# A Mamba-2 scan feeding a hard-swish MLP: the last chunk's mixing in halves, a sum of weights moved, a state sum left out

## The chip, the cores and the metric

The kernel runs on one core of a Trainium2 chip. The metric is the device time of one execution in microseconds (us). A core has five engines with a queue of instructions each: PE (TensorE, matrix products), DVE (VectorE), ACT (ScalarE), POOL (GpSimd) and SP (SyncE, which issues most DMA transfers here). Each runs its own queue in order and waits on semaphores for the others. PE's results go to PSUM, which has eight banks; everything else is in SBUF.

## The reference

A chunked state-space scan over 4 batches x 8 heads x 768 tokens (head size 32, state size 16), whose result is turned to 3072 tokens x 256 and put through an MLP with a hard-swish between its products. The inputs x, a, B and C are float32, the two weights float64.

```python
for c in range(nc):
    cum = np.cumsum(la, axis=-1)
    L = np.exp(cum[:, :, :, None] - cum[:, :, None, :]) * causal
    CB = np.einsum('bhin,bhjn->bhij', Cc, Bc)
    y_intra = np.einsum('bhij,bhjd->bhid', CB * L, xc)
    y_inter = np.einsum('bhin,bhnd->bhid', Cc, state) * np.exp(cum)[..., None]
    y[:, :, sl] = y_intra + y_inter
    state = decay_full * state + np.sum(Bx, axis=2)
...
h = x @ w_in
g = h * np.clip(h + 3.0, 0.0, 6.0) / 6.0
return g @ w_out
```

The state after the last chunk is used by nothing.

## The kernel before

The 768 tokens are taken in NC = 6 chunks of 128, all batches at once, so that a chunk has 512 columns. The main loop at the end of the kernel has a block k for each chunk: it multiplies chunk k through the MLP, and between those products it places the scan of chunk c = k + 1 and the preparation of chunk ahead = k + 2. The order of the instructions on each engine is the order of the calls in the code; it is written out by hand.

**The scan of a chunk.** A chunk is cut in two halves a of 64 tokens, and an inner step runs from half 0 to half 1. `scores(c)` makes C times B for both (tile cb), and then calls `into_state`, which multiplies x by B with its decays (tile bs), one sum for each half, into the banks of y (line L555). `multiply(c)` first has ACT copy the second half's sum to the tile adds (`take`, L571), then DVE multiplies cb into the decays L (L584), and between them `new_state` makes the state between the halves (mid). `renew(c)` makes the state that the next chunk starts from, out of mid and adds; it isn't called for the last chunk. `mix(c, parts)` multiplies L by x for four heads at each part u (L610), and at the end adds what the state between the halves gives (`from_state`, L516). On PE a mixing is 128 small matmuls of L610 and 32 of L516, each with its weight load, since a float32 product is made of two. Then `split_y(c)` cuts the result y into the parts high (ACT, L671), low (DVE, L674) and gap (DVE, L677), from which the first product of the MLP is made.

**A block of the MLP, k of 1 to 5.** For each of 16 slices f of the hidden width, `lead` multiplies the gaps (L683) and then scales its bank: for an even f on ACT (L699), for an odd one on DVE (L696). `follow` adds the products of high and low (L683 too), and ACT and DVE make the hard-swish gT of it (L706, L707). A lead stands two slices ahead of its follow. The first two leads of the next block are put at the end of the block before: in block 0 ahead of its last two out-products, in blocks 1 to 4 at unit 12.

The second product, g @ w_out, has a form with seven products in place of eight, which needs sums of quarters of g (made by POOL, L779) and four sums of quarters of w_out. `weight_sums` makes the latter on DVE, one at each `next(sums)` (L761, 128 x 1024 each), in the order t3, t2, t4 and t1 in place; each but the first uses an earlier one. Block 0 makes its second product the plain way (`first_out`, L734) while the weights still come in. In blocks 1 to 4 `wide_units` makes it in units with a yield between them; after a unit, by its number i, the loop puts in the steps of the scan. Its tiles are wa, wb and wc (L860), a unit has 8 or 16 matmuls. Block 5 uses `out_units` (oa and ob, L793).

**What stands where before.** In block 0: after the out-products (i, b) = (2, 3) come scores, multiply and renew of chunk 1, decays of chunk 2, and two sums of w_out; after (3, 1) come mix and split_y of chunk 1 (`results`), then the third sum, and decays. The fourth sum is made in block 1. In blocks 1 to 4: scores and multiply after unit 2; after unit 6 mix and split_y together, apart from chunk TURN = 3 (block 2), where the first part of mix is put after unit 6 and the second, with split_y, after unit 7. Unit 7 is the second part of a product into wb; its code also has DVE turn back a quarter of the result (L874). For block 4 c = 5 and ahead = 6, so that nothing is loaded or prepared there.

The nested conditions of the loop after unit 6, with the names as above:

```python
                if i == 6 and c == TURN:
                    mix(c, (0,))
                if i == (7 if c == TURN else 6):
                    results(c, (1,) if c == TURN else range(2))
```

Of the kernel before, what the change touches and what calls it, by code (L numbers as in the profile page):

```python
# [21 lines left out]
def kernel(  # L22
# [29 lines left out]
    NC = S // P  # L52
# [34 lines left out]
    TURN = 3  # L87
# [290 lines left out]
    def diff_exp(c, b):  # L378
        if c not in Ls:
            new_decays(c)  # L380
        nc.scalar.activation(Ls[c][:, b], ds.pop((c, b)), AF.Exp)
# [139 lines left out]
    def own_banks(c):  # L521

        both = [ps_y.tile([P, 2, NB, HT], FP32, name=f"y{u}", tag=f"y{u}") for u in range(2)]
        ys[c] = {(0, u): both[u][:, 0] for u in range(2)}
        sps[c] = [both[a if c else 1 - a][:, 1] for a in range(2)]
        if c:
            from_state(c, 0)

    def scores(c):

        bT, cT, _ = bTs[c]
        cbs[c] = [ps.tile([P, NB, 2, HT], FP32, name="cb", tag=f"f{q}") for q in range(NQ)]
        if c not in ys:
            own_banks(c)
        for b in range(NB):
            for a, rows in enumerate(HALF):  # L540
                for q in range(NQ):
                    pair = slice(32 * q, 32 * q + 32)
                    nc.tensor.matmul(  # L543
                        out=cbs[c][q][rows, b], lhsT=bT[pair, b, rows],
                        rhs=cT[pair, b, :, rows], start=(b == 0), stop=True,
                        tile_position=(32 * q, a * HT), skip_group_check=True)
        into_state(c, 0, 1)

    def into_state(c, *halves):
        xt, bs = xts[c], bss[c]  # L550
        for b in range(NB):
            for q in range(NQ):
                hs = slice(b * NH + 2 * q, b * NH + 2 * q + 2)
                for a in halves:
                    nc.tensor.matmul(  # L555
                        out=sps[c][a][32 * q:32 * q + 32, b],
                        lhsT=bs[HALF[a], hs].rearrange("s h n -> s (h n)"),
                        rhs=xt[HALF[a], hs].rearrange("s h d -> s (h d)"),
                        start=(c == 0 and b == 0), stop=True, tile_position=(a * HT, 32 * q),
                        skip_group_check=True)  # L560

    def new_state(t, sp, old):
        for u in range(2):
            ds_ = slice(u * D, (u + 1) * D)
            nc.vector.scalar_tensor_tensor(
                out=t[:, :, ds_], in0=sp[:, :, ds_], scalar=parity[:, u:u + 1],
                in1=old[:, :, ds_], op0=ALU.mult, op1=ALU.add)

    def take(c):
        adds[c] = att.tile([P, NB, 2 * D], FP32, name="adds", bufs=1)  # L570
        nc.scalar.copy(out=adds[c], in_=sps[c][1])  # L571

    def multiply(c):

        take(c)
        mids[c] = mid = att.tile([P, NB, 2 * D], FP32, name="mid", bufs=1)
        if c == 0:
            for t in range(2):
                nc.scalar.activation(
                    mid[:, :, t * D:(t + 1) * D], sps[c][0][:, :, t * D:(t + 1) * D], AF.Copy,  # L580
                    scale=parity[:, t:t + 1])
        for q in range(NQ):
            hs = slice(2 * q, 2 * q + 2)
            nc.vector.tensor_tensor(  # L584
                out=Ls[c][:, :, hs], in0=Ls[c][:, :, hs], in1=cbs[c][q], op=ALU.mult)
            if c and q == 1:
                new_state(mid, sps[c][0], tmps[c])
# [349 lines left out]
    def results(c, parts=range(2)):  # L937
        mix(c, parts)
        split_y(c)
# [18 lines left out]
    def weights(i, n):  # L958
        for _ in range(n):
            next(parts[i], None)  # L960
# [63 lines left out]
    for k in range(NC):  # L1024
        gTs[k] = ffn.tile([P, NF, TB], FP32, name="gT")
        c, ahead = k + 1, k + 2
        if k == 0:
            for f in range(NF):
                mlp_in(k, f)
                for i in weave.get(f, []):  # L1030
                    weights(i, 1)
                if f in (6, 8):
                    diff_exp(c, f // 2 - 3)
            load_bc(ahead)
            weights(NP + 1, 1)
            weights(NP + 3, 1)
            weights(NP + 2, 3)
            sums = weight_sums()
            for i in range(NP):
                for b in range(NB):  # L1040
                    first_out(b, i, c)
                    if (i, b) == (0, 0):
                        weights(NP + 3, 1)
                        weights(NP + 2, 1)
                        weights(NP + 3, 3)
                        rows(ahead)
                    elif (i, b) == (1, 0):
                        for j in range(NP - 1):
                            high_w(j)
                        for j in range(2):  # L1050
                            low_w(j)
                            gap_w(j)
                    elif (i, b) == (2, 0):
                        turn(c, 1)
                        wake(c)
                        turn(c, 0)
                        low_w(2)
                        gap_w(2)
                        high_w(NP - 1)
                        for p in range(2):  # L1060
                            conceal(ahead, p)
                    elif (i, b) == (2, 3):
                        scores(c)
                        multiply(c)
                        renew(c)
                        decay_ends(ahead, 0)
                        decay_ends(ahead, 1)
                        next(sums)
                        next(sums)
                    elif (i, b) == (3, 1):  # L1070
                        results(c)
                        next(sums)
                        decay_ends(ahead, 2)
                        load_x(ahead)
            rows(ahead + 1)
            continue
        for f in range(NF):
            if f == 0:
                if ahead < NC:
                    load_bc(ahead)  # L1080
                if 1 < k and c < NC:
                    carry(c)
                turns = turn_parts(c) if c < TURN else iter(())
            if f + 2 < NF:
                lead(k, f + 2)
            follow(k, f)
            if k == 1:
                if f in (0, 2):
                    low_w(NP - 1, f // 2)
                if f in (4, 6):  # L1090
                    gap_w(NP - 1, f // 2 - 2)
                if f in (1, 3):
                    decay(c, NB - 1, range(f // 2 * HU, (f // 2 + 1) * HU))
                if f == 3:
                    ends(c, NB - 1)
                    from_start(c)
                    carry(c)
            if f in (4, 8) and ahead < NC:
                conceal(ahead, f // 4 - 1)
            if f in (5, 7, 8):  # L1100
                next(turns, None)
            if f == 9 and c < TURN:
                turn(c, 1)
            if f in (4, 8, 12):
                g_sums(k, f // 2 - 2)
        for i, _ in enumerate((wide_units if c < NC else out_units)(k)):
            if i == 0:
                g_sums(k, NJ - 2)
                if k == 1:
                    next(sums)  # L1110
            if c < NC:
                if i == 1 and c == NC - 1:
                    own_banks(c)
                if i == 2:
                    scores(c)
                    multiply(c)
                    if c < NC - 1:
                        renew(c)
                if ahead < NC and 2 <= i < 6:
                    decay_ends(ahead, i - 2)  # L1120
                if i == 6 and c == TURN:
                    mix(c, (0,))
                if i == (7 if c == TURN else 6):
                    results(c, (1,) if c == TURN else range(2))
                    if ahead < NC:
                        load_x(ahead)
                        from_start(ahead)
                    if ahead + 1 < NC:
                        rows(ahead + 1)
                if i == 9 and TURN <= ahead < NC:  # L1130
                    turn_all(ahead)
                if i == 12:
                    lead(c, 0)
                    lead(c, 1)
# [30 lines left out]
```

## Time and profile before

| what | value |
|---|---|
| median of 3 runs | 347.82 us (347.5 to 348.46) |
| the profiled execution: time / its span | 349.42 us / 347.7 us |
| mean granted PE clock | 0.995 |
| PE busy (matmuls) | 335.3 us, 96% of the span |
| DVE / ACT / POOL busy | 220.1 / 173.5 / 141.5 us |
| chain that ended last, shares | PE 89%, DVE 5%, DMA 3%, the rest 3% |
| DMA | 24.89 MB, mean 72 GB/s |

The span runs from the first to the last instruction, the execution's time takes in what lies around it. "Busy" is the time in which an engine had an instruction of its own at work. The chain is followed back from the last instruction, at each step to what released it. "issue" stands for time in which an engine waited for nothing that the profile shows. The page's row of the granted clock, one digit for each of 40 slices of 8.7 us, beside the shares of PE:

```
PE   6799999998999999999999999999999979999996
PEclk9999999999999999999999999999999989999999
```

A digit is a tenth; 9 is 90% or more. By the cut at each block's first wide product, blocks 1, 2 and 3 take 51.55, 51.93 and 51.57 us.

### The profile page before, as it was taken

The numbers are of one execution on the slowest core, as the hardware profiler recorded it, in microseconds if no ns is written. First come the engines' busy times: TensorE is split into PE (matmuls) and PEld (weight loads), VectorE is DVE, ScalarE is ACT, GpSimd is POOL, SyncE is SP. The second block draws the span as 40 slices with busy tenths as digits, with TensorE's granted clock in tenths as the row PEclk, the third lists the DMA queues.
The fourth block names the chain that finished last, engine by engine and source line by source line (L and its number), as shares of the span: only waits on it lengthen the run. The fifth ranks groups of instructions, "written<-read, shape, count | busy, mean of one in ns | idle before, by whom it ended". The sixth has DMA issues, their size and how long they took to land.

```text
span 347.7 us, 8242 instructions
## 1 busy us (share of the span) xinstructions
PE 335.3 (96%) x3408; PEld 267.8 (77%) x3408; DVE 220.1 (63%) x357; ACT 173.5 (50%) x360; POOL 141.5 (41%) x139
## 2 busy tenths in 40 slices
PE   6799999998999999999999999999999979999996
PEld 2554458887778888888888888888887868888996
DVE  6689999988697648774448674438663332576011
ACT  4768888737874651663741663741662010565000
POOL 3300000291299913299512299510399100089500
PEclk9999999999999999999999999999999989999999
DMA  7898969106930066241047242051200000200000
GB/s 170 160 340 170 248 194 173 33 2 94 198 59 17 5 96 135 34 62 42 2 60 164 35 58 50 4 67 23 34 4 0 2 8 11 32 16 0 2 31 30
DMA packets 91605, 24.89 MB, mean 72 GB/s; under 512 B 84208, under 2 KB 87952, under 8 KB 91056
## 3 DMA queue, kind: packets, MB, share of 16 engines
q1 hardware_dynamic: 87184, 23.06, 34.5%
q10 hardware_dynamic: 4384, 1.31, 1.6%
q8 instruction: 26, 0.43, 0.5%
q14 instruction: 11, 0.09, 0.1%
HBM read 21.07 MB, written 3.29 MB: 70 GB/s over the span
## 4 chain that ended last, share of the span: by engine, by line
PE 89%; DVE 5%; DMA 3%; issue 1%; ACT 1%; SPq 1%; DVEq 0%
PE h L683 31%; PE wb L860 13%; PE wc L860 8%; PE h L635 8%; PE wa L860 8%; PE o L734 6%; PE oa L793 4%; PE ob L793 4%; PE y L610 2%; PE y L516 2%; PE cb L543 2%; DMA raw<-in_moe_w_in_dram 2%; DVE L L584 1%; DMA pairs<-in_C_dram 1%; PE y L555 1%
## 5 line engine op out<-in xcount | busy, mean ns | idle before, releaser
L707 DVE SCALAR_TENSOR_TENSOR gT<-gT,h 128x512 f32<-128x512 f32 x80 | 54.9, 687 | 32.1 <-ACT gT L706 29.3
L706 ACT ACTIVATE gT<-h,half_up 128x512 f32<-128x512 f32 x80 | 55.1, 690 | 33.3 <-PE h L683 33.1
L779 POOL TENSOR_TENSOR s<-gT 128x512 f32<-128x512 f32 x20 | 25.7, 1287 | 69.9 <-DVE gT L707 69.9
L683 PE MATMUL h<-gap,w_gap 128*128 128x512 f32 x160 | 51.8, 409 | 1.0 <-DVE gap L677 1.0
L683 PE MATMUL h<-high,w_high 128*128 128x512 f32 x160 | 50.7, 398 | 0.1
L683 PE MATMUL h<-low,w_low 128*128 128x512 f32 x160 | 50.3, 395 | 0.0
L699 ACT ACTIVATE h<-h 128x512 f32<-128x512 f32 x40 | 23.6, 589 | 31.3 <-PE h L683 31.3
L683 PEld LDWEIGHTS h<-gap,w_gap 128*128 128x128 f32 x160 | 29.9, 188 | 8.0 <-DVE gap L677 1.4
L683 PEld LDWEIGHTS h<-high,w_high 128*128 128x128 f32 x160 | 29.5, 188 | 8.6 <-DVE h L696 2.0
L683 PEld LDWEIGHTS h<-low,w_low 128*128 128x128 f32 x160 | 30.1, 188 | 7.2
L860 PE MATMUL wb<-s,w_out 128*128 128x256 f32 x128 | 32.0, 395 | 0.0
L401 ACT ACTIVATE L<-L,cum_n 128x64 f32<-128x64 f32 x128 | 31.6, 337 | 0.7 <-POOL L L162 0.7
L734 PE MATMUL o<-w_out,gT 128*128 128x256 f32 x128 | 28.7, 381 | 0.0
L696 DVE TENSOR_SCALAR h<-h 128x512 f32<-128x512 f32 x40 | 27.7, 692 | 1.2 <-PE h L683 1.2
L419 POOL TENSOR_TENSOR tmp<-state,eto 128x256 f32<-128x256 f32 x5 | 3.6, 716 | 60.5 <-ACT eto L405 60.3
L635 PE MATMUL h<-yT,w 128*128 128x512 f32 x64 | 27.7, 594 | 0.0
L860 PEld LDWEIGHTS wb<-s,w_out 128*128 128x128 f32 x128 | 24.7, 196 | 3.9
L779 POOL TENSOR_TENSOR s<-s,gT 128x512 f32<-128x512 f32 x20 | 26.9, 1343 | 1.6
L584 DVE TENSOR_TENSOR L<-L,cb 128x512 f32<-128x512 f32 x24 | 15.3, 682 | 19.1 <-PE cb L543 16.3
L734 PEld LDWEIGHTS o<-w_out,gT 128*128 128x128 f32 x128 | 24.1, 190 | 3.8 <-issue 0.5
L412 POOL TENSOR_TENSOR bs<-B,L 128x128 f32<-128x128 f32 x24 | 12.7, 542 | 33.0 <-ACT L L401 27.9
L779 POOL TENSOR_TENSOR gT<-gT 128x512 f32<-128x512 f32 x20 | 25.8, 1291 | 0.0
(141 smaller groups left out, 534.7 us busy)
## 6 DMA issues: line engine op xcount, KB each, us to landing
raw<-in_moe_w_out_dram SPq DMA_DIRECT2D x4, 1024.0 KB
L<-cum_d SPq DMA_DIRECT2D x8, 512.0 KB
xt<-in_x_dram SPq DMA_DIRECT2D x6, 512.0 KB
raw<-in_moe_w_in_dram SPq DMA_DIRECT2D x3, 1024.0 KB
out_dram<-back SPq DMA_DIRECT2D x128, 16.0 KB
eto<-cum_e SPq DMA_DIRECT2D x20, 64.0 KB
B<-in_B_dram SPq DMA_DIRECT2D x5, 256.0 KB
raw<-in_moe_w_in_dram ACTq DMA_DIRECT2D x1, 1024.0 KB
```

Source lines behind the costliest of these rows:

```text
L401: nc.scalar.activation(Ls[c][:, b, h], Ls[c][:, b, h], AF.Exp, bias=cum_n[:, c, g:g + 1])
L584: nc.vector.tensor_tensor(out=Ls[c][:, :, hs], in0=Ls[c][:, :, hs], in1=cbs[c][q], op=ALU.mult)
L635: nc.tensor.matmul(out=h.rearrange("p r i -> p (r i)"), lhsT=first_in[f // FP][:, j, f % FP * P:(f % FP + 1) * P], rhs=yTs[k][:, j], start ...
L683: nc.tensor.matmul(out=h, lhsT=w[:, j, f * P:(f + 1) * P], rhs=y[:, j], start=(start and j == 0), stop=True, skip_group_check=True)
L696: nc.vector.tensor_scalar(out=h, in0=h, scalar1=-Z / UP, scalar2=None, op0=ALU.mult)
L699: nc.scalar.mul(h, h, -Z / UP)
L706: nc.scalar.activation(g, h, AF.Relu, bias=half_up, scale=UP * UP / 6.0)
L707: nc.vector.scalar_tensor_tensor(out=g, in0=g, scalar=UP, in1=h, op0=ALU.min, op1=ALU.mult)
L734: nc.tensor.matmul(out=o[:, b % 2], lhsT=gTs[0][:, f, b * P:(b + 1) * P], rhs=w_out[:, f], start=(f == 0 and b % 2 == 0), stop=True, skip_ ...
L779: nc.gpsimd.tensor_tensor(out=o, in0=p_, in1=q_, op=op)
L793: nc.tensor.matmul(out=bank[:, slot], lhsT=lhs[:, j], rhs=rhs[:, j], start=(clear and j == 0), stop=True, skip_group_check=True)
L860: nc.tensor.matmul(out=bank[:, slot], lhsT=lhs[:, j], rhs=rhs[:, j], start=(clear and j == 0), stop=True, skip_group_check=True)
```

## The change

Three edits. First, `apart` takes in the last chunk: in block 4 the first part of chunk 5's mixing is put after unit 6 and the second, with split_y, after unit 7, as block 2 has it. Second, for the last chunk `into_state` makes only the first half's sum, and `multiply` leaves `take` out: 16 small float32 products and one ACT copy less. The second half's sum would go into a state that nothing uses. Third, in block 0 only one sum of w_out is made ahead of the mixing and split_y of chunk 1, and two behind it.

```diff
-        into_state(c, 0, 1)
+        into_state(c, *range(2 if c < NC - 1 else 1))
...
     def multiply(c):
-        take(c)
+        if c < NC - 1:
+            take(c)
...
                         decay_ends(ahead, 1)
                         next(sums)
-                        next(sums)
                     elif (i, b) == (3, 1):
                         results(c)
                         next(sums)
+                        next(sums)
                         decay_ends(ahead, 2)
...
+                apart = c in (TURN, NC - 1)
-                if i == 6 and c == TURN:
+                if i == 6 and apart:
                     mix(c, (0,))
-                if i == (7 if c == TURN else 6):
-                    results(c, (1,) if c == TURN else range(2))
+                if i == (7 if apart else 6):
+                    results(c, (1,) if apart else range(2))
```

## The prediction

> **What bounds the kernel now.** TensorE: the page has PE busy 335.3 of 347.7 us, and PE work is 89% of the chain that ended last. So I read next what PE waits for, then the span cut at each block's first out-product, then the chain of block 4 beside block 2's, and last VectorE's (DVE's) timeline at the end of block 0. The waits of PE:
>
> ```profile
> PE y L516 <- issue: 1.8, 1, 1.8
> ...
> PE h L683 <- DVE gap L677: 1.0, 1, 1.0
> ```
>
> Of the seven waits these two lie in code that the diff touches; the other five (2.1, 2.0, 1.0, 0.6, 0.5) all end before 21 us, ahead of the first edit. Blocks 3 and 4 as stretches:
>
> ```profile
> 212.13:263.70 51.57, 51.57 (x530) 43.01 (x529) 30.17 (x53) 25.62 (x64) 23.90 (x23) 1.00 0.18 27
> 263.70:319.40 55.70, 53.87 (x531) 44.32 (x530) 26.14 (x45) 17.67 (x31) 20.18 (x17) 0.97 0.07 11
> ```
>
> The columns are length, busy time of PE, of its weight loads, of DVE, ACT, POOL, then the granted clock. With one PE record more, block 4 takes 4.13 us more than block 3, and it alone has a clock under 1.00. The chain (start, us, what), block 2's mixing, which is already in halves, above block 4's:
>
> ```profile
> 175.00 0.79 PE y L610 x53
> 175.79 1.92 PE wb L860 x8
> 177.72 0.79 PE y L610 x53
> 178.50 0.62 PE y L516 x32
> 179.13 3.65 PE wc L860 x16
> ...
> 278.86 1.41 PE y L610 x90
> 280.27 0.62 PE y L516 x30
> 280.89 1.83 issue
> 282.72 0.27 PE y L516 x2
> 282.99 3.30 PE wb L860 x8
> 286.29 3.77 PE wc L860 x16
> ```
>
> Two products short of its end, block 4's mixing stops for 1.83 us with nothing to wait for, and the eight wb that follow take 3.30 us instead of 1.92. Microsecond windows (length, PE busy, clock, DMA share, GB/s) show what lies around it:
>
> ```profile
> 279.00:280.00 1.00, 1.00 (x124) 1.00 0.09 16
> 281.00:282.00 1.00, 0.00 (x0) 1.00 0.00 0
> 284.00:285.00 1.00, 1.00 (x4) 0.50 0.00 0
> ```
>
> The transfer in 279:280 is one 16 KB packet of the instruction queue q8: it starts at about 279.80 and takes 9.2% of 16 engines' microsecond, 1.47 us. The page has 26 such packets for 6,816 PE instructions, 262 each, which I take for the block. I read the stop as PE out of instructions: a mixing is 128 + 32 matmuls and as many weight loads, 320 instructions in 2.03 us, more than one block of code. The one other "issue" wait, 0.5 us in the first mixing, looks alike: its packet takes 5.5% of 16 us, 0.88 us from about 18.03, and PE goes on at 20.29, 1.38 us after it landed; here it is 282.72 - 281.27 = 1.45.
>
> **Edit 1, the halves, with edit 2's share in it.** From the mixing to wa's second part block 4 needs 290.06 - 278.86 = 11.20 us; block 2, in halves, 182.78 - 175.00 = 7.78; blocks 1 and 3, in one piece, 7.42 and 7.41. So the halves cost 0.36 us (each return from small tiles to wide ones costs some 0.19: wb 1.92 against 1.73, wc 3.65 against 3.45), and what there is to win is 11.20 - 7.78 = 3.42. Of it the half clock is 1.71 (3.41 us from about 283.3 at 0.50: the windows 283:284 to 286:287 read 0.69, 0.50, 0.50, 0.60), and 1.71 is the stop of 1.83 less the 0.36, with 0.24 of smaller losses about it.
> Does the stop go? It came after 128 + 31 loads and 128 + 30 matmuls, 317 instructions, so that block of code began some 55 into the mixing. Edit 2 takes 64 instructions (32 matmuls and their loads) out shortly ahead, so it begins at about 119, near the end of half one's 128. Then come 9, the unit's 16 and half two's 192: 217 of 262; the next block is first needed 45 further on, where 16 last 1.73 us: 1.9 + 1.4 + 4.9 = 8.2 us after this one began. Before, block start to resumption took some 3.5 us (279.2 to 282.7). It goes, with 4 us to spare. By halving alone the next block would be needed 173 instructions into half two, after 0.4 + 1.9 + 1.1 = 3.4 us, a draw. I take no stop. Ends: 3.42 won, and 0.36 lost if there is none to be won.
> [...]
> Behind half two, split_y comes one unit later: in block 2 half two ends at 179.1 and the first lead is at 187.96, with ACT and DVE needing 4 x 0.38 and 4 x 0.42 + 2 x 0.69 = 4.6 us even in line. Block 4 issues no loads there (no chunk is ahead); the only DVE work moved in front is one turn back, 0.44. DVE and ACT there are idle for 5.5 us (290.50 waited so long). Cost nothing; without that cover up to the 1.9 of the unit.
>
> **Edit 2, no second state sum.** L555 takes 0.79 us on PE in block 4 for 64 matmuls; half go: 0.40. Ends: 0, if one half alone runs no faster, and 0.79. The ACT copy L571 (0.37) goes too; ACT had been idle 6.83 us before it: nothing.
>
> **Edit 3, one weight sum moved behind the parts of y.** On DVE, at the end of block 0:
>
> ```profile
> 79.59 1.32 DVE L761 TENSOR_TENSOR t<-t,w_out 128x1024 f32<-128x1024 f32 x1
> 80.83 0.74 DVE L674 TENSOR_TENSOR low<-y,high 128x256 fp32r<-128x256 f32 x2
> ...
> 83.00 0.92 DVE L677 SCALAR_TENSOR_TENSOR gap<-low,high 128x512 fp32r<-128x512 f32 x1
> 83.84 1.21 DVE L761 TENSOR_TENSOR t<-w_out,t 128x1024 f32<-128x1024 f32 x1
> 84.98 0.70 DVE L696 TENSOR_SCALAR h<-h 128x512 f32<-128x512 f32 x1
> ```
>
> PE stands from 82.97 to 83.97 for the second gap. Without the sum at 79.59 the parts start when ACT has the first high: its four start at 79.67 and take 1.26, so the first is there at 80.05. Moved from 80.83 to 80.10 the row of parts ends at 83.19 instead of 83.92, and at 82.96 if the last gap takes 0.69 as the one at 81.61 did. PE's stand falls to between 0.27 and nothing: 0.73 to 1.00 won, I take 0.85.
> What is late next: DVE now has two sums before h of f = 1, which ends at 83.1 + 1.3 + 1.2 + 0.7 = 86.3. PE wants it when it comes to high of f = 1, at 87.51, now 86.66: 0.3 to spare, then 0.8 before gT of f = 0 (DVE idled 2.29 there). Nothing; but at 2.22 each, as the fourth sum takes at 110.0, h would end 1.9 later and PE lose 1.6. ACT and POOL are not moved; no queue is passed.
>
> **Sum.** On the profiled execution, 347.7 of span in 349.42 us: 0.85 + 0.40 + 3.42 = 4.67, to 344.75. But the median shown is 347.82, 1.60 under that execution, and the half clock is worth 1.71. The two need not come together: PE stood 2.0 us at 12.9 to 14.9 at clock 1.00 throughout, longer than here. So I take it that the median has the stop but not the half clock: 0.85 + 0.40 + 1.71 = 2.96, **344.9 us**; with the ends above (0.73 to 1.00, 0 to 0.79) and a stop 0.3 shorter or longer without the profiler, 344.1 to 345.7.
> [...]
>
> **Rivals.** A measurement of this kernel tells about 0.3% (1.0 us) from no change.
> - Half clock in the median too: 347.82 - 4.67 = **343.2**. For it: the profile has it. Against: the 1.60.
> - No stop in unprofiled runs, or the change doesn't take it away (the block begins elsewhere than I count): 0.85 + 0.40 - 0.36 = 0.89 won, **346.9**. For it: the count rests on 317 instructions and a mean of 262; against: the spare 4 us.
> - Slower: the stop moves into half two and the half clock, which the median has not, now falls there. 0.36 + 1.71 - 0.40 - 0.85 = 0.82 lost, **348.6**. It decides once the next block arrives after half two, that is if edit 2 shifted nothing and fetching took over 3.4 us.
>
> **Chances.** Forecast 0.52, half clock 0.28, no stop won 0.13, slower 0.07. Range: both first cases with their ends, and what lies between them and the third, 342.8 to 346.6. Faster by over 0.3% takes the first two: 0.80; within 0.3%: the third and half of the last, 0.16; slower 0.04.
>
> **What would show it.** Right: PE's waits have no "issue" in block 4 and at most 0.3 for gap; the clock is 1.00 throughout; the stretch of block 4 is 55.70 - 3.42 - 0.40 = 51.9; L555 has 352 matmuls, L571 five copies; the profiled execution falls by 4.7 and so comes near the new median. Wrong: an issue wait in half two, a wait of PE on h (L696) near 86, or L555 at 0.79 still in block 4.

## The result, and the profile after

The changed kernel takes 345.91 us (median of 22 executions, 344.85 to 349.40), the kernel before, executed beside it, 348.55 (22, 347.01 to 351.97). The ratio, worked out over the executions and not as the quotient of the two medians, is 0.9919, with a 95% interval of 0.9891 to 0.9947: 0.8% faster. The forecast was 344.9 against 347.82, a ratio of 0.9916. The measured 345.91 lies inside the whole range (342.8 to 346.6) and 0.2 above the forecast's own ends (344.1 to 345.7), beside a kernel before that came out 0.73 higher as well.

The profiled execution of the changed kernel took 349.17 us with a span of 347.4, hardly less than the 347.7 of before; its mean granted clock is 0.979. So it has to be read stretch by stretch. First the waits of PE in it, all of them:

```profile
PE d L352 <- POOL head L184: 2.1, 1, 2.1
PE cb L543 <- DVE cT L488: 1.9, 1, 1.9
PE d L364 <- DVE split L293: 1.2, 1, 1.2
PE c_ps L329 <- DVE L L585: 0.4, 1, 0.4
```

Both waits that the edits aimed at, the issue wait in y L516 and the one for gap, are gone; no new wait has come in their place. The windows of blocks 3 and 4 (length, PE, weight loads, DVE, ACT, POOL, clock, DMA share, GB/s), and the chain from block 4's mixing on:

```profile
215.31:266.86 51.55, 51.55 (x529) 43.00 (x529) 30.14 (x53) 25.60 (x64) 23.85 (x23) 1.00 0.18 27
266.86:319.14 52.28, 52.18 (x499) 42.79 (x498) 26.14 (x45) 17.18 (x30) 20.18 (x17) 1.00 0.07 11
```

```profile
282.02 0.79 PE y L611 x53
282.81 1.92 PE wb L861 x8
284.73 0.79 PE y L611 x53
285.52 0.62 PE y L516 x32
286.15 3.65 PE wc L861 x16
289.80 3.45 PE wa L861 x16
```

Block 4 went from 55.70 to 52.28, and from the mixing to wa's second part it is 289.80 - 282.02 = 7.78 us, block 2's figure to the hundredth. DVE at the end of block 0 (start, us, what):

```profile
84.08 0.93 DVE L675 TENSOR_TENSOR low<-y,high 128x256 fp32r<-128x256 f32 x2 [0.32 <-ACT high L672]
...
86.43 0.69 DVE L678 SCALAR_TENSOR_TENSOR gap<-low,high 128x512 fp32r<-128x512 f32 x1
87.04 1.22 DVE L762 TENSOR_TENSOR t<-t,w_out 128x1024 f32<-128x1024 f32 x1
...
89.54 0.68 DVE L697 TENSOR_SCALAR h<-h 128x512 f32<-128x512 f32 x1
```

DVE now waits for ACT's first high instead of being late for it, the second gap is ready at 87.12 (86.43 + 0.69), in time for PE, which does not stop there, and the two sums run behind. What this execution lost, it lost at the start. One window of PE (length, busy, clock, DMA share, GB/s) and the first product's piece of the chain:

```profile
20.00:22.00 2.00, 2.00 (x87) 0.50 1.02 418
```

```profile
24.14 30.28 PE h L636 x64
```

From 15.7 to 29.4 us it ran at half clock, and L635's 64 products (L636 after), 27.66 us before, took 30.28. No edit lies there, and other executions of the same kernel, at a clock of 1.00, have spans of 343.1 to 344.8.

### The profile page after: what moved, and what is told of

It is laid out like the page before. It is cut to its first block, busy times and chain, and to the rows that moved or that the text cites. A ratio compares the mean times of both kernels' runs of the same rounds, so it can differ in the third digit from the quotient of the medians.

```text
span 347.4 us, 8177 instructions
## 1 busy us (share of the span) xinstructions
PE 338.4 (97%) x3376; PEld 269.0 (77%) x3376; DVE 220.3 (63%) x357; ACT 173.3 (50%) x359; POOL 142.4 (41%) x139
## 4 chain that ended last, share of the span: by engine, by line
PE 93%; DMA 3%; DVE 2%; ACT 1%; SPq 0%; issue 0%; DVEq 0%
PE h L684 31%; PE wb L861 12%; PE h L636 9%; PE wc L861 8%; PE o L735 8%; PE wa L861 8%; PE oa L794 4%; PE ob L794 4%; PE y L611 3%; PE y L516 2%; PE cb L543 2%; DMA raw<-in_moe_w_in_dram 2%; DMA pairs<-in_C_dram 1%; PE y L555 1%; PE d L506 1%; PE t_ps L438 1%
## 5 line engine op out<-in xcount | busy, mean ns | idle before, releaser
L861 PE MATMUL wb<-s,w_out 128*128 128x256 f32 x128 | 30.7, 382 | 0.0
L636 PE MATMUL h<-yT,w 128*128 128x512 f32 x64 | 30.3, 638 | 0.0
L861 PEld LDWEIGHTS wb<-s,w_out 128*128 128x128 f32 x128 | 24.0, 190 | 3.6
L412 POOL TENSOR_TENSOR bs<-B,L 128x128 f32<-128x128 f32 x24 | 14.0, 597 | 30.8 <-ACT L L401 26.1
L636 PEld LDWEIGHTS h<-yT,w 128*128 128x128 f32 x64 | 13.0, 205 | 16.6 <-issue 14.5
```

Of the source, the lines that this page charges most:

```text
L636: nc.tensor.matmul(out=h.rearrange("p r i -> p (r i)"), lhsT=first_in[f // FP][:, j, f % FP * P:(f % FP + 1) * P], rhs=yTs[k][:, j], start ...
L861: nc.tensor.matmul(out=bank[:, slot], lhsT=lhs[:, j], rhs=rhs[:, j], start=(clear and j == 0), stop=True, skip_group_check=True)
```

## The experiments

The changed lines are shown for each; the line numbers shift by a few. Times are of whole executions; the last column is the median span of those whose mean granted clock was 0.999 or more, so that what the half clock does is left out.

| run | median us | ratio to before (95%) | span at full clock (of so many) |
|---|---|---|---|
| the change | 345.91 | 0.9919 (0.9891 to 0.9947) | 343.9 (13 of 22) |
| e0, before itself | 349.90 | 1.0014 (0.9982 to 1.0047) | 347.3 (1 of 12) |
| e1, sums as before | 346.97 | 0.9918 (0.9890 to 0.9947) | 344.95 (8 of 12) |
| e2, halves alone | 347.69 | 0.9950 (0.9918 to 0.9981) | 345.2 (5 of 12) |
| e3, no state sum alone | 347.18 | 0.9923 (0.9894 to 0.9951) | 344.55 (4 of 12) |
| e4, edits 2 and 3, last mixing in one piece | 345.33 | 0.9914 (0.9879 to 0.9948) | 343.6 (5 of 8) |
| e5, all mixings in one piece | 345.19 | 0.9904 (0.9869 to 0.9940) | 343.1 (6 of 12) |
| e6, before with 34 instructions in block 3 | 350.77 | 1.0031 (1.0000 to 1.0062) | 346.7 (3 of 12) |
| e7, e4 with 64 instructions in block 4 | 349.02 | 0.9990 (0.9957 to 1.0023) | 346.3 (5 of 12) |
| f1, e5 with 144 instructions in the first wait | 351.45 | 1.0047 (1.0011 to 1.0083) | none of 12 |
| f2, e5 with one wide product there | 344.80 | 0.9873 (0.9817 to 0.9930) | 343.05 (4 of 6) |
| f3, the change again | 345.98 | 0.9913 (0.9882 to 0.9945) | 343.9 (7 of 12) |
| f4, f2 with 128 instructions at 6.5 us | 351.38 | 1.0051 (1.0019 to 1.0084) | none of 8 |

Beside e0 to e3 the kernel before had 346.45 in 8 of 35 executions, beside e4 to e7 346.4 in 11 of 31, beside f1 to f3 345.9 in 10 of 23, beside f4 346.9 in 3 of 12. So the same kernel differs by up to 1.0 from one of these sets to another, and a smaller difference between runs of two sets shows nothing by itself.

**e0: the kernel before itself.**

> The kernel before itself, to see the granted clock of each of its executions. If half clock comes by chance after the stop in block 4, its executions fall into those with a clock of 1.00 (span near 346) and those below, 1.7 us or more longer; the profile shows the issue wait of some 1.8 us in block 4 and the wait of 1.0 for gap again. If the stop were a matter of one execution alone, the issue wait would be missing here.

```profile
283.10 1.59 issue
284.69 0.27 PE y L516 x2
284.96 1.92 PE wb L860 x8
```

In the chain of this profile the stop is there, 1.59 us, at the same two products from the end, but the wb that follow take 1.92: no half clock. Block 4 takes 53.79 us here against 55.70. So the stop belongs to the kernel, the half clock behind it to some of its executions. A span near 346 was expected at full clock, and the executions beside it have 346.45. But full clock is rarer than I had thought: 1 of these 12 executions, and with those beside the runs 33 of 113.

**e1: edit 3 undone.**

```diff
 # the changed kernel
                         next(sums)
+                        next(sums)
                     elif (i, b) == (3, 1):
                         results(c)
                         next(sums)
-                        next(sums)
```

> The changed kernel with edit 3 undone: two sums of w_out ahead of y's parts again. Theory (each edit has its own wait): PE waits some 1.0 us for the second gap near 83, no issue wait in block 4, and executions at a clock of 1.00 take 0.7 to 1.0 us more than the changed kernel's, 344.0 to 344.6 of span. Rival (the sums are covered in either order, the wait moves on to h of f = 1): within 0.3 us of the changed kernel.

```profile
PE h L684 <- DVE gap L678: 1.0, 1, 1.0
```

The wait for gap is back. From the first product of chunk 1's mixing to the first wide product of block 1 PE takes 30.64 us here and 29.69 in the changed kernel, 0.95 less; the six profiles with the old order of the sums have 30.64 to 30.66, those with the new one 29.68 to 29.72 (apart from f4, with a short stop there). The spans at full clock differ by 344.95 - 343.9 = 1.05, but come from two sets. The rival, within 0.3, is out by the profiles. Whole executions don't show this gain: the ratios are 0.9918 here and 0.9919 for the change. Its block 4 takes 52.29.

**e2: edit 1 alone.**

```diff
 # the kernel before
-                if i == 6 and c == TURN:
+                apart = c in (TURN, NC - 1)
+                if i == 6 and apart:
                     mix(c, (0,))
-                if i == (7 if c == TURN else 6):
-                    results(c, (1,) if c == TURN else range(2))
+                if i == (7 if apart else 6):
+                    results(c, (1,) if apart else range(2))
```

> The kernel before with edit 1 alone: the last chunk's mixing in halves, the second state sum kept. Theory (blocks of some 256 instructions; PE stops where the next is not there yet): the block that began 61 into the mixing still does, so the next one is needed some 19 instructions before half two's end, about 3.4 us later: a stop of 0 to 0.4 us there, in from_state. Rival (the stop belongs to 160 products run in one piece): no stop. Both: wait of 1.0 for gap stays; block 4 takes 3.4 us less than in a profile with half clock there.

```profile
281.77 0.79 PE y L610 x53
282.56 0.62 PE y L516 x32
283.18 3.65 PE wc L860 x16
```

No stop in block 4, which takes 52.29 us. The halves alone do it, at the end of the range that both theories allowed: this run told nothing apart. What it did tell, beside e1: with the second state sum or without it, block 4 in halves takes the same 52.29.

By the trace it is a draw: the packet of code had landed at 281.44, and PE came to that block's first instruction at 282.83, 1.39 us later, while after a stop in blocks 3 and 4 it goes on 1.36 to 1.49 us after the landing. In the changed kernel the packet landed at 284.98 and PE came at 290.93, 5.95 later: some 4.5 us to spare.

**e3: edit 2 alone.** The kernel leaves out the state after the last chunk, as the change does.

```diff
 # the kernel before
-        into_state(c, 0, 1)
+        into_state(c, *range(2 if c < NC - 1 else 1))
...
-        take(c)
+        if c < NC - 1:
+            take(c)
```

> The kernel before with edit 2 alone: no second state sum for the last chunk, the mixing in one piece. Theory (blocks of code): 64 instructions fewer move the start of the block from 61 to 125 into the mixing, the next is needed 61 after its end: no issue wait, and block 4 takes 51.5 us, 0.4 less than in the changed kernel, since the halves' own cost is saved. Rival (the stop belongs to 160 products in one piece): the stop of 1.8 us stays at the end of the mixing, block 4 takes 53.5 without half clock and 55.3 with it.

```profile
272.13 0.58 PE y L555 x32
272.71 1.93 PE wb L861 x8
274.63 0.10 issue
274.73 3.69 PE wc L861 x16
...
280.58 1.41 PE y L611 x90
281.99 0.62 PE y L516 x32
282.62 1.92 PE wb L861 x8
```

In its chain the mixing is in one piece and runs through: 1.41 + 0.62, then wb at 1.92. Block 4 takes 51.91 us, 0.37 less than in the changed kernel (the 51.5 expected had counted 0.40 for the state sum). So 160 products in one piece did not stop PE here, and the halves aren't needed once 64 instructions are gone ahead of them. The upper lines show the state sum's own worth: 0.58 for 0.79, but then 0.10 of issue and 3.69 for 3.58 of wc: from L555 to the end of wc the pieces add up to 6.30 us here and in e2.

**e4 and e5: the change without the halves, and block 2 without them too.** Both leave out the last state, as the change does.

```diff
 # the kernel before with edits 2 and 3; e4 keeps its lines, e5 has
-                if i == 6 and c == TURN:
-                    mix(c, (0,))
-                if i == (7 if c == TURN else 6):
-                    results(c, (1,) if c == TURN else range(2))
+                if i == 6:
+                    results(c, range(2))
```

> Edits 2 and 3 without edit 1: the last chunk's mixing stays in one piece. Theory (edit 2's shift alone removes the stop, the halves cost 0.36): no issue wait in block 4, no wait for gap, executions at a clock of 1.00 at 343.5 of span, 0.4 under the changed kernel's 343.9. Rival (the halves are what keeps the stop away once edit 3 has moved the timing): a stop of 1.6 to 1.8 at the mixing's end, 345.3.

> As the run before, and block 2's mixing in one piece too. Theory (the place of the blocks of code decides): counted in the trace, a block begins 113 instructions into that mixing and the next is needed 50 after its end, so no stop there either; 0.36 more saved, 343.1 at a clock of 1.00. Rival (a mixing in one piece beside block 2's turning of the next chunk stops or delays something): an issue wait or a wait of the leads in block 2, 343.5 or more.

No issue wait in blocks 1 to 5 of either. e4's block 4 takes 51.93, 0.35 less than the changed kernel's; e5's block 2 takes 51.56 instead of 51.92. At full clock e4 has 343.6 and e5 343.1, against 343.9 in other sets: the direction and for e5 the size that were expected, but too small to be told between sets. Over whole executions the intervals of both ratios hold the change's 0.9919, so it is the blocks that show the gain.

**e6 and e7: the stop moved, and the stop brought back.** Both write small products to a bank that the next product clears; e7 leaves out the last state.

```diff
 # e6: the kernel before, PAD_AT, PAD = (3, 8), 17; e7: e4 with (4, 8), 32
+        if (k, f) == PAD_AT:
+            for _ in range(PAD):
+                nc.tensor.matmul(
+                    out=h[:, :HT], lhsT=ident_h, rhs=hide, start=True, stop=True,
+                    skip_group_check=True)
         in_product(h, w_gap, gaps[k], f, start=True)
```

> The kernel before with 17 small products (34 PE instructions with their loads) put ahead of the first product of slice 8 in block 3, written to a bank that the product then clears. Theory (blocks of 256 instructions, counted from the stop): in block 3 a block of code now begins 61 instructions into the mixing, as it did in block 4, so the stop of 1.6 to 1.8 us appears at the end of block 3's mixing; in block 4 the place is now 27 into it, and the stop is gone or under 0.5. Rival (the stop belongs to block 4 by what is around it, such as the banks taken early, or the missing transfers): it stays in block 4 and block 3 has none.

> Edits 2 and 3 with the mixing in one piece, and 32 small products (64 PE instructions) put ahead of slice 8's first product in block 4, into a bank that is then cleared. Theory (only the count of instructions ahead of the mixing matters): with the 64 put back the stop of 1.6 to 1.8 us returns at the end of block 4's mixing, though the state sum is still left out. Rival (it was the state sum itself, its bank or its ACT copy, that made the stop): no issue wait there.

The chain of e6, in block 3:

```profile
229.48 0.62 PE y L517 x30
230.10 1.42 issue
231.52 0.27 PE y L517 x2
```

and of e7, in block 4:

```profile
282.48 0.62 PE y L517 x30
283.10 1.37 issue
284.47 0.27 PE y L517 x2
```

34 instructions in block 3 bring the stop there, to the same two products from the end, and leave block 4 without one (51.92 us). 64 instructions of another kind, put in 30 us ahead, bring it back to block 4, though the state sum is gone. So neither block 4, nor the state sum, nor the length of the mixing by itself made it: where the mixing lies among the blocks of code did, and the count of PE instructions ahead sets that. Counted in the traces, PE stops after its 5,057th instruction in e6 and its 6,081st in e7, as in the kernel before; the first stop of the kernel, in the first mixing, comes after the 705th. These are multiples of 256 apart. Shorter issue waits of 0.2 to 0.4 us in block 1's state sum, in e1, e2, e3 and e6, come after the 2,497th, on the same count; the profiles of the kernel before and the changed one have none there, so this place stopped PE in some of the profiled executions only. The sizes, 1.42 in e6 and 1.37 in e7, fell short of the 1.6 to 1.8 expected; the packets of code took 0.95 and 0.94 us here, 1.47 where the stop was 1.83 and 1.26 where it was 1.59. The added products cost time of their own: the stretches that hold them take 0.57 us more in e6 (52.50 for 51.93) and 1.03 more in e7 (52.60 for 51.57).

**f1, f2 and f4: the start.** In the changed kernel's profile the half clock lies at the start, so these aim there; all leave out the last state. What differs from e5:

```diff
 # f1
+    fill = ps.tile([P, NB * P], FP32, name="d", tag="f3")
+    for _ in range(72):
+        nc.tensor.matmul(
+            out=fill[:HT, :HT], lhsT=ident_h[:, :HT], rhs=hide, start=True, stop=True,
+            tile_position=(0, 0), skip_group_check=True)
     scores(0)
 # f2 and f4
+    busy(1, ps.tile([P, NB * P], FP32, name="d", tag="f3"))
     scores(0)
 # f4 alone
+    for _ in range(64):
+        nc.tensor.matmul(
+            out=ds[0, 0][:HT, 0], lhsT=ident_h[:, :HT], rhs=hide, start=True, stop=True,
+            tile_position=(0, 0), skip_group_check=True)
     for b in range(2):
         mask_again(0, b)
```

> Edits 2 and 3, all mixings in one piece, and 72 small products (144 PE instructions, about 1.6 us) in PE's 1.9 us wait ahead of the first scores, into a bank that is then cleared. Theory (blocks of code, and half clock after an idle stretch): the blocks now begin near the wait's end and in the gap before the first mixing, so the issue wait of 0.5 to 1.3 us in the first mixing goes and none comes elsewhere, and fewer executions have a clock under 1.00 than half of them; at a clock of 1.00 the span is 342.0 to 342.7 against 343.1 without the filling. Rival (the start is bounded by its loads, and the half clock is set by something else): span and share of low clocks as without it, 343.1 and half.

> As the run before, but one wide product (2 PE matmuls, 1.1 us) in that wait in place of 72 small ones. Theory: the idle stretch falls to 0.9 us, so fewer low clocks; but the blocks of code are moved by 4 instructions only, so the issue wait of 0.5 to 1.3 us in the first mixing stays, and the span at a clock of 1.00 is near 343.1. Rival: if it equals the run before, the filling and not the place of the blocks is what counts.

> The changed kernel again, on the same chip as the two runs before: 343.9 at a clock of 1.00, a ratio near 0.992, and no issue wait in block 4.

> The kernel with one wide filler (edits 2 and 3, mixings in one piece) and 64 small products (128 PE instructions, some 1.5 us) ahead of the first decays' products, at 6.5 us, into a bank that is then cleared. With the filler's 4 this moves the blocks of code by 132. Counted from the stops (after the 705th PE instruction and every 256 from there) the first blocks then end just ahead of the first scores, behind the first state sum and 240 into the first mixing. Theory (a stop needs a block that is entered and used up within about 4 us): the block entered ahead of the scores is called for in PE's wait, the next in the gap behind the sums, so the wait of 1.2 in the first mixing goes or falls under 0.5, and at a clock of 1.00 the span is 342.0 to 342.6 against 343.05. Rival (at the start the transfers of the data hold the code up wherever the blocks lie): a stop of 0.5 to 1.3 us appears at another place among the first scores and mixing, 343 or more. Both: no issue wait later.

f1 and f4 missed. PE's timeline of f1, the pieces that stop:

```profile
18.43 0.30 PE L555 MATMUL y<-xt,bs 64*32 64x64 f32 x4 [1.26 <-issue]
...
24.46 0.67 PE L611 MATMUL y<-L,xt 64*32 64x64 f32 x27 [1.24 <-issue]
```

and of f4:

```profile
19.53 0.42 PE L329 MATMUL c_ps<-ident,pre 32*128 32x32 f32 x2 [1.77 <-issue]
...
27.20 0.64 PE L611 MATMUL y<-L,xt 64*32 64x64 f32 x21 [2.13 <-issue]
```

Two stops where there had been one, again after instructions 705 and 961, and no execution at full clock: f1 lost 0.5% to the kernel before, f4 too. The places of the stops were as counted; what failed is that the next block would come in time there: the 4 us or so that I had allowed for it, from block 4, were not enough. In f1 the packet for the block after instruction 961 started 3.7 us after PE had entered the block before it (18.43 to 22.17), in f4 5.2 us after (19.52 to 24.72); in block 4 of the kernel before it was 0.8 (279.01 to 279.80). From 10 to 30 us the DMA engines are nearly full (shares of 0.97 and 0.90 in f1's windows of ten). f4's rival, that these transfers hold the code up, fits and foretold a stop at another place, though a smaller one (0.5 to 1.3); that they are the cause isn't shown. The 144 and 132 instructions more at the start put the 961st into the first mixing. f2 adds only four. Its waits of PE:

```profile
PE y L611 <- issue: 1.2, 1, 1.2
...
PE cb L543 <- DVE cT L488: 0.9, 1, 0.9
```

As expected, the idle stretch ahead of the scores is 0.9 for 1.9, the stop in the first mixing stays, and the span at full clock is 343.05. Its ratio of 0.9873 (0.9817 to 0.9930) is the lowest of all, but from six executions and with an interval that still holds the change's 0.9919; that the filler lowers the share of low clocks (2 of 6 against 6 of 12 in e5) they are too few to show. f3, the changed kernel on the same chip, gave 0.9913, as before.

## Why the prediction was right, and which terms were off

- **The stop is PE out of code, and the change takes it away: right.** e6 and e7 move it at will by the count alone. The stops come after 705, 961, 5,057 and 6,081 instructions, whole multiples of 256 apart, and at the end of the mixings in blocks 3 and 4 PE stood for 1.37 (e7), 1.42 (e6), 1.59 (e0) and 1.83 us (before).
- **Where the next block is needed: right.** Some 4.5 us to spare with edit 2, where I had 4, and a draw for the halves alone (e2), which ended without a stop. The mean of 262 that I took for a block is 256 by the count of the stops, so it began 61 and not 55 into the mixing. I put the removal down to both edits; e3 shows that edit 2 does it alone, and that the halves only cost.
- **The halves' cost of 0.36: right**, 52.28 - 51.91 = 0.37.
- **The state sum's 0.40: mis-sized, 0.** L555 fell by 0.21, not by half, and the units behind it gave that back (e1 and e2, both 52.29), so block 4 came to 52.28 and not 51.9. The lower end of 0 was the right one. What edit 2 is worth is the 64 instructions.
- **The wait for gap, 0.85: 0.95** (the stretch from chunk 1's mixing to block 1, e1 against the change), nearly all of the wait of 1.0. The sums behind it cost nothing, as said: no wait on h of f = 1.
- **The stop without half clock, 1.71 net: 1.51**, 53.79 in e0 less 52.28. Together 0.95 + 1.51 = 2.46 where I had 2.96. The spans at full clock differ by 346.45 - 343.9 = 2.55 with the kernel before of e0 to e3, and by 345.9 - 343.9 = 2.0 where both ran in one set (f3).
- **"The median has the stop but not the half clock": wrong as a statement on the kernel before.** For the three executions shown it probably held by luck: their clocks aren't on record, but of 113 executions of this kernel 19 took under 348.0 us, 16 of them at full clock, and their median was 347.82. Of all 113, 80 were below full clock, and beside the changed kernel the median was 348.55. Of the changed kernel 20 of 34 were at full clock. So the medians differ by 2.64, which is in part stop and wait and in part half clock, and that the ratio of 0.9919 comes so near to 0.9916 is in part luck: terms too large (the state sum, the stop) met one left out.
- **The profiled execution would fall by 4.7: wrong.** It fell by 0.3. Block 4 gave its 3.42, the gap its 1.0, and the start, where I foresaw nothing, took some 4 back by the half clock from 15.7 to 29.4. So the sign of a clock at 1.00 throughout failed too, in this execution.
- **Two ends of the range were added wrongly**: with the ends named, the forecast's lower one is 347.82 - (1.00 + 0.79 + 1.71 + 0.30) = 344.0, not 344.1, and that of the half clock case 342.3, not 342.8. Neither matters for the result.

What stays open: which of the low clocks of the kernel before come from block 4 and which from the start. An execution tells only its mean clock. Of the three profiles with the stop in block 4 (before, e0, e7) one had half clock behind it.

## What to carry to other kernels

Where a burst of several hundred short instructions stops for nothing that the profile shows, count the instructions of that engine up to the stop and look at the instruction queue's packets: here the place of the burst among the blocks of code decided; 64 instructions fewer ahead took the stop of block 4 away (e3), 34 more moved it to block 3 (e6), and 64 more brought it back (e7), and the added ones cost their own time (1.03 us for the 64 of e7). Count before cutting the burst up: here the cut cost 0.37 us for what the count had already given. In one profile a stop of 1.83 us on PE was followed by 3.41 us at half clock, which cost 1.71 us more, so compare executions by their granted clock before comparing medians.

## What the runs showed of the hardware

- PE went on 1.2 to 1.6 us after its packet of code had landed, at every stop of 0.3 us and more: 281.27 to 282.72 in the kernel before, 283.33 to 284.69 in e0, 230.03 to 231.52 in e6, 16.99 to 18.43 in f1; the ends are 1.24 (18.96 to 20.20 in e2) and 1.57 (25.63 to 27.20 in f4).
- Half clock came in pieces of 3.41 us or whole multiples of it: one in block 4 before (283.38 to 286.79), two in e3's start (15.35 to 22.18), four in the changed kernel's start (15.71 to 29.36). In each trace the changes of the clock lie whole multiples of 3.41 us apart (81 of them up to block 4's fall before, 6.90 to 283.38), on a grid that begins elsewhere in each execution: its first line lies 0.07 us into the span of the profile before and 2.06 into that of the changed kernel.
- How long PE stood idle within one piece of that grid went with the clock of the next piece. The stops and the wait ahead of the first scores, by the traces:

| profile | piece of the grid, us | PE idle in it, us | clock of the next piece |
|---|---|---|---|
| before, block 4 | 279.97 to 283.38 | 1.83 | 0.50 |
| e0, block 4 | 282.58 to 286.00 | 1.59 | 1.00 |
| e6, block 3 | 229.93 to 233.34 | 1.42 | 1.00 |
| e7, block 4 | 282.67 to 286.08 | 1.37 | 1.00 |
| the change, start | 12.30 to 15.71 | 1.85 | 0.50 |
| e0, start | 12.93 to 16.34 | 1.77 | 1.00 |
| before, start | 10.31 to 13.73, then 13.73 to 17.14 | 0.88, then 1.43 | 1.00, 1.00 |

Over all 14 profiles, each of the 14 pieces at full clock with 1.83 us or more of idle time was followed by half clock; of those with 1.77 or less three were (0.90 in e7, 0.98 in e0, 1.26 in f1), all with the small products of the first scores or the first mixing in them. So the stop of 1.83 in block 4 is at the lower end of those 14, and the idle 2.0 us from 12.9 to 14.9 that kept full clock in the kernel before was parted by the grid at 13.73. Why those three fell stays open.
